# Loading q and k of the first batch in two parts, by halves of the queries, under a newly searched plan

## The chip, the cores and the metric

The kernel runs on one core of one Trainium2 chip. The metric is the device time of one execution in microseconds (us). Engines are named as in the profile: PE (TensorE, matmul), DVE (VectorE), ACT (ScalarE), POOL (GpSimd), SP (SyncE, which issues the DMAs here).

## The reference

Block-causal attention of 8 batches with 8 heads, 576 positions and 64 features, in blocks of 64, and behind it a feed-forward layer on the 4608 tokens:

```python
scores = scale * np.matmul(q, k.transpose(0, 1, 3, 2))
scores = np.where(block_i >= block_j, scores, -1e9)
scores = scores - np.max(scores, axis=-1, keepdims=True)
attn = np.exp(scores)
attn = attn / (np.sum(attn, axis=-1, keepdims=True) + 1e-09)
x = (attn @ v).transpose(0, 2, 1, 3).reshape(B * S, H * D)     # 4608 x 512
h = x @ w_in                                                   # 512 x 2048
sp = np.where(h > 20.0, h, np.log1p(np.exp(np.minimum(h, 20.0))))
out = (h * np.tanh(sp)) @ w_out                                # 2048 x 512
```

q, k and v are float32; w_in and w_out are float64, which the kernel turns into float32 itself from the two 32-bit words of each number.

## The kernel before

**Tiles.** The tokens are worked through in 16 tiles, two per batch. Batch 0 is cut into 384 queries and then 192 (`HALVES[0]`), each later batch in the same two sizes. Heads go in pairs, four pairs per batch. The two products of the feed-forward layer are called fc1 (`m1`, L1597) and fc2 (`m2`, L1702). Most matrix operands are kept as two float16 parts, a high part (`hi`) and the rest (`lo`); three products of parts give one product of the values.

**Batch 0** is loaded by `load_own` (q and k of a pair at L799, v at L811, into `Et`) and is computed in float32 by `attend`: scores by query (`by_query`, L1008 and L1020) only for the largest of each row (DVE, L1038 and L1045), then scores again (L1079), less the largest (L1118), the exponential (L1136, ACT) and the product with v (L1151). Both halves take q and k by `st["A"]`, the list of the loads that they wait for.

**Later batches** are loaded by `load_pair` and split there into parts on DVE, ACT or POOL: `QH`, `KH`, `VH` at L916 and L920, `QL`, `KL`, `VO` at L924. `attend_pair` computes them: scores (L1217, L1229), largest (L1258), exponential (L1292), its parts `P` (L1336, L1342), DMA transposes to `PT`, and the product with v (L1419). `weigh` divides by the sums (L1482, L1483) and splits the result into the parts of x (`xt`; lo at L1510 on DVE), and a DMA transpose (L1552) gives fc1's input `x`.

**Weights.** `weight` loads w_in and w_out in groups (L574), joins the pairs of words on DVE (L583 once and L600 twice per piece), takes sums of squares on ACT, and makes hi (L633 on ACT or L640 on DVE) and lo (L691 on DVE). w_out is staged in `Gt`, the buffer that later holds g, the input of fc2. So `split`, which turns g into hi (L1658 on ACT or L1667 on DVE) and lo (L1673 on DVE), starts for the first tile only when all of w_out has been turned.

**What sets the order.** The program first records all operations with their engines, times and dependences. `Plan.order` then schedules them by a list, each with a due time, and writes them out by planned start. The due times stand in the table `DUE`, with entries for the weights ("w"), the factors of a batch ("batch"), the loads ("load") and the steps of each tile ("tile"). Some casts may go to one of several engines, and the plan picks it. Each engine then runs its instructions in that order.

Of the kernel before, what the change touches and what calls it, by code (L numbers as in the profile page):

```python
# [20 lines left out]
P = 128  # L21
# [11 lines left out]
    "load": (
        (208.5, -15.5, 753.5, -60),
        (11, 400.5, 274, -70.5),
        (340, 173.5, 586.5, 293.5),
        (578, 514, 523.5, 553.5),
        (424.5, 386.5, 195, 638.5),
        (322.5, 411.5, 596, 331),
        (584, 710.5, 581, 634),  # L40
        (438, 791, 455, 590),
        (680, 545.5, 578, 593),
    ),
    "tile": (
        (-224.5, -143.5, 54.5, -83, -49.5, 18.5, -40.5, -39.5,
         390, 274.5, 399.5, 301, 31.5, -9.5, 456.5,
         285.5, 377.5, 60.5, 43.5, 313, 373, 541.5),
# [6 lines left out]
        (556, 28.5, 43.5, 267.5, 271, 246.5, 357, 631,
         78.5, 354.5, 335.5, 437.5, 368.5, -81, 131.5,
         346.5, 484, 458, 450.5, -175.5, 259, -164),
        (499, 409, 666, 287.5, 361.5, 346, 584.5, 335.5,
         410.5, 580.5, 432, 328.5, 456, -17, 480.5,
         803, 688, 639.5, 703, 535, 795.5, 716),
        (375.5, 527, 655.5, 634.5, 283.5, 770, 564.5, 346,  # L60
         425, 319, 858, 637.5, 494.5, 350.5, 351.5,
         929, 577, 311.5, 608.5, 548, 597.5, 159),
        (306.5, 431, 500, 483.5, 571.5, 1003.5, 781.5, 774,
         365, 672, 681.5, 628.5, 660.5, 502.5, 476,
         685, 408, 626.5, 522.5, 753.5, 818.5, 612),
        (433.5, 846, 424.5, 516.5, 719, 718, 500.5, 370.5,
         291, 514, 709.5, 645.5, 739.5, 11.5, 1009.5,
         871.5, 834, 978.5, 960.5, -56, 497.5, 184),
        (439.5, 516, 278.5, 523, 696, 408, 425.5, 656,
         339.5, 783, 867, 642.5, 943, 496, 707.5,  # L70
         635.5, 556.5, 683, 526.5, 854.5, 1014, 576),
        (593.5, 821.5, 469.5, 708, 1061.5, 887, 1110.5, 767.5,
         934, 825.5, 611.5, 831.5, 550.5, 183, 942,
         665, 465, 1008.5, 532, -321, 616, -132.5),
        (795.5, 1021, 1212.5, 461, 796.5, 965, 738, 804.5,
         543.5, 1015, 850.5, 1107.5, 800, 351, 1100,
         641.5, 827, 830, 518.5, 520, 1157, 626),
        (840, 631.5, 963.5, 1028, 1010, 859, 729.5, 885.5,
         715.5, 640, 1192, 1173, 978.5, -42, 1032.5,
         604.5, 1306, 972.5, 1169.5, 147.5, 750.5, -88.5),  # L80
        (1060.5, 775, 744, 721.5, 1067, 849, 818, 691.5,
         706.5, 899.5, 717.5, 943.5, 1099.5, -7.5, 741,
         670, 1056.5, 1241.5, 789.5, 1082.5, 638, 882.5),
        (1025, 1352.5, 1013, 610, 788.5, 728, 1114.5, 1102,
         968.5, 1007, 846, 931, 1091, -24, 740,
         1131.5, 719.5, 1054.5, 854.5, -2.5, 938, 423.5),
# [1785 lines left out]
```

## Time and profile before

| | |
|---|---|
| median of 3 runs | 999.4 us (996.87 to 999.95) |
| the profiled execution | 998.63 us, its span 996.9 us |
| granted PE clock, mean | 0.995 |
| PE busy | 973.1 us (98%) |
| DVE busy | 668.5 us (67%) |
| ACT busy | 663.4 us (67%) |
| POOL busy | 115.0 us (12%) |

The span is what the trace covers; 1.7 us of the execution lie around it. The shares of busy time are means over the whole span: the first 150 us, in which batch 0 is attended to and the weights are turned, differ from the rest. In a row of PE's timeline several instructions of one kind stand together, and a number in brackets is the idle time ahead of them and what ended it. A granted clock of 1.00 is 2.4 GHz, 0.50 is 1.2 GHz.

### The profile page before, as it was taken

The page shows a single profiled execution, that of the slowest core. Times are in us where ns is not written, and L with a number is a line of the kernel's source. Part 1 is how long each engine was busy: PE and PEld are TensorE (multiplying, and loading weights), DVE is VectorE, ACT ScalarE, POOL GpSimd, SP SyncE. Part 2 cuts the span into 40 slices and gives each one's busy share as a digit, 9 for nine tenths or more (in the row PEclk, how much of TensorE's full clock was granted, in tenths as well). Part 3 has the DMA queues.
Part 4 walks back from the last instruction along what each step waited for, and adds up shares of the span by engine and source line. Part 5 has one row for each costly group of instructions (what it writes and reads, how often), then busy time and mean ns, then how long its engine had stood idle before and what let it go on. Part 6 is the DMA issues. An engine that isn't in the chain of part 4 may idle for free.

```text
span 996.9 us, 25050 instructions
## 1 busy us (share of the span) xinstructions
PE 973.1 (98%) x10576; PEld 722.2 (72%) x10576; DVE 668.5 (67%) x1411; ACT 663.4 (67%) x1062; POOL 115.0 (12%) x166
## 2 busy tenths in 40 slices
PE   6999879999999999999999999999999999999998
PEld 5677557786777867777677866777677776876787
DVE  5999999779899687564798378965389636420210
ACT  3769987769768678656788678887668835432221
POOL 0011232011112002000120031010011000000000
PEclk9999979999999999999999999999999999999999
DMA  9863755796677745472668377873277333420000
GB/s 324 270 174 113 183 97 140 152 180 149 119 165 163 163 100 110 91 161 50 143 151 171 71 135 137 156 148 50 57 173 146 76 69 82 82 57 1 25 17 25
DMA packets 275505, 121.56 MB, mean 122 GB/s; under 512 B 221376, under 2 KB 261568, under 8 KB 275392
## 3 DMA queue, kind: packets, MB, share of 16 engines
q1 hardware_dynamic: 275392, 119.97, 55.4%
q8 instruction: 82, 1.34, 0.5%
q14 instruction: 31, 0.25, 0.1%
HBM read 56.10 MB, written 9.44 MB: 66 GB/s over the span
## 4 chain that ended last, share of the span: by engine, by line
PE 86%; DVE 9%; DMA 2%; issue 1%; ACT 1%; SPq 1%; ACTq 0%; DVEq 0%
PE acc L1702 37%; PE acc L1597 35%; PE u L1419 7%; PE ss L1217 6%; DVE Gt L600 1%; DVE wo_h L600 1%; DMA x<-xt 1%; DVE wo_l L691 1%; DMA wo_l<-in_w_in_dram 1%; DVE PT L1045 1%; PE u L1151 1%; DVE pv L1258 1%; DMA PT<-P 1%; DVE P L1342 0%; DVE wi_l L691 0%
## 5 line engine op out<-in xcount | busy, mean ns | idle before, releaser
L1597 PE MATMUL acc<-x,wi_h 128*128 128x192 f16 (+1 forms) x2048 | 394.8, 286 | 4.1 <-ACT Et L1626 2.7
L1702 PE MATMUL acc<-Gt,wo_h 128*128 128x192 f16 (+1 forms) x2048 | 386.1, 287 | 0.2 <-DVE Gt L1673 0.2
L1702 PE MATMUL acc<-Gt,wo_l 128*128 128x192 f16 (+1 forms) x1024 | 293.7, 287 | 0.0
L1597 PE MATMUL acc<-x,wi_l 128*128 128x192 f16 (+1 forms) x1024 | 293.0, 286 | 0.0
L1597 PEld LDWEIGHTS <-wi_h 128*128 128x128 f16 x2048 | 191.1, 98 | 86.0 <-issue 8.5
L1702 PEld LDWEIGHTS <-wo_h 128*128 128x128 f16 x2048 | 187.6, 98 | 50.2 <-issue 3.3
L1626 ACT ACTIVATE Et<-acc,bv 128x384 f32<-128x384 f32 x192 | 109.4, 579 | 118.1 <-PE acc L1597 116.7
L1292 ACT ACTIVATE pe<-ss,pv 128x192 f32<-128x192 f32 (+1 forms) x280 | 148.1, 606 | 12.8 <-DVE pv L1266 8.2
L1673 DVE SCALAR_TENSOR_TENSOR Gt<-Et,bv,Gt 128x1536 f16<-128x1536 f32 (+1 forms) x64 | 91.3, 1432 | 78.7 <-ACT Gt L1658 78.3
L1258 DVE TENSOR_REDUCE pv<-ss 128x2 f32<-128x384 f32 (+4 forms) x140 | 106.0, 789 | 41.8 <-PE ss L1229 41.5
L1702 PEld LDWEIGHTS <-wo_l 128*128 128x128 f16 x1024 | 100.4, 98 | 34.0 <-issue 1.1
L1597 PEld LDWEIGHTS <-wi_l 128*128 128x128 f16 x1024 | 100.2, 98 | 33.1
L1342 DVE TENSOR_TENSOR P<-pe,P 128x256 f16<-128x256 f32 (+1 forms) x168 | 110.8, 700 | 14.9 <-ACT P L1336 13.3
L1292 ACT ACT_TABLE_LOAD x59 | 75.7, 1283 | 12.5 <-DVE pv L1266 7.8
L1336 POOL CAST P<-pe 128x256 f16<-128x256 f32 (+3 forms) x81 | 60.3, 777 | 201.9 <-DMA PT<-P 79.2
L1626 ACT ACT_TABLE_LOAD x62 | 79.5, 1283 | 1.1
L1419 PEld LDWEIGHTS <-PT 128*128 128x128 f16 x2128 | 72.8, 98 | 5.1 <-issue 0.6
L1419 PE MATMUL u<-VH,PT 128*128 128x65 f16 x1344 | 74.3, 193 | 0.0
L1658 ACT ACTIVATE Gt<-Et,bv 128x768 f16<-128x768 f32 (+1 forms) x51 | 63.4, 1248 | 15.9 <-PE acc L1702 14.0
L1419 PE MATMUL u<-VO,PT 128*128 128x64 f16 x784 | 72.6, 193 | 0.0
L1741 ACT ACTIVATE ot<-acc,bv 128x192 f32<-128x192 f32 (+1 forms) x46 | 21.1, 487 | 66.8 <-PE acc L1702 52.9
L1217 PEld LDWEIGHTS <-QH 64*128 64x128 f16 x896 | 27.4, 95 | 28.7 <-issue 13.5
(126 smaller groups left out, 978.7 us busy)
## 6 DMA issues: line engine op xcount, KB each, us to landing
out_dram<-ot SPq DMA_DIRECT2D x48, 192.0 KB, 2.0
wo_l<-in_w_in_dram SPq DMA_DIRECT2D x8, 1024.0 KB, 7.3
Gt<-in_w_out_dram SPq DMA_DIRECT2D x16, 512.0 KB, 4.5
kl<-in_v_dram SPq DMA_DIRECT2D x28, 288.0 KB, 3.1
ql<-in_q_dram SPq DMA_DIRECT2D x28, 288.0 KB, 3.0
kl<-in_k_dram SPq DMA_DIRECT2D x28, 288.0 KB, 3.1
VL<-in_v_dram SPq DMA_DIRECT2D x28, 192.0 KB, 2.9
VL<-in_v_dram SPq DMA_DIRECT2D x28, 96.0 KB, 3.1
```

What stands on the lines that cost most here:

```text
L1217: nc.tensor.matmul(ss[:, 512 * a + col : 512 * a + col + n], lhsT=m[q_][hs, at : at + P], rhs=m[k_][hs, key : key + n], start=first, stop= ...
L1258: nc.vector.reduce_max(out=mx[:, c], in_=ss[:, :, c0:c1], axis=mybir.AxisListType.X)
L1292: nc.scalar.activation(pe[ex[r].slot][:, cols], ss_[S0[r].slot % NSS][:, cols], AF.Exp, scale=esc, bias=mx[:, c, a : a + 1],)
L1336: op(out=h, in_=x)
L1342: nc.vector.tensor_sub(l, x, h)
L1419: nc.tensor.matmul(out, lhsT=p_, rhs=v_, start=first, stop=True, skip_group_check=True,)
L1597: nc.tensor.matmul(pt, lhsT=w[:, d, f * P : (f + 1) * P], rhs=x[:, d, :], start=k == 0 and d == 0 and z == 0, stop=d == NP - 1 and z == 2, ...
L1626: nc.scalar.activation(Et[:, (self.i * NG + g) % NE, j : j + K, 0:n], acc_[c.slot % NACC][:, 0 : K * n].rearrange("p (k n) -> p k n", k=K) ...
L1658: lambda g_hi=g_hi, ev=ev: nc.scalar.activation(g_hi, ev, AF.Copy, scale=self.s_g),
L1673: lambda g_hi=g_hi, g_lo=g_lo, ev=ev: nc.vector.scalar_tensor_tensor(out=g_lo, in0=ev, scalar=self.s_g, in1=g_hi, op0=ALU.mult, op1=ALU.su ...
L1702: nc.tensor.matmul(pt, lhsT=w[:, f, o * P : (o + 1) * P], rhs=g, start=k == 0 and f == 0 and z == 0, stop=f == NF - 1 and z == 2, skip_gro ...
L1741: evac(lambda o, i, s: nc.scalar.activation(o, i, AF.Copy, scale=s))
```

## The change

`load_own` issues two transfers for q and two for k of each pair of batch 0: columns 0 to 384 (the first half of the queries and the keys that they see) and columns 384 to 576. The second part carries a due time of its own, the first entry of the pair in tile 1. `attend` waits in the first half for the first parts only, and in the second for both. v is loaded as before. The whole table `DUE` is new, so that the order on every engine is another one.

```diff
-    "w": ((-53.5, -7.5, 92, 14.5), (645, 263, 668.5, 387)),
+    "w": ((-85, 131, 174, 350.5), (416, 560.5, 362.5, 233.5)),
...
-        ins = [
-            add(
-                "sp",
-                dma(P * S * 4),
-                lambda t=t, src=src: nc.sync.dma_start(out=t, in_=src),
-            )
-            for t, src in ((m["QF"], qT[0, rows]), (m["KF"][:, 0:S], kT[0, rows]))
-        ]
+        parts = []
+        for h, (c0, c1) in enumerate(HALVES[0]):
+            plan.part("load", 0, p)
+            if h:
+                plan.part("tile", 1, 2 * p)
+            parts.append(
+                [
+                    add(
+                        "sp",
+                        dma(P * (c1 - c0) * 4),
+                        lambda t=t, src=src, cs=slice(c0, c1): nc.sync.dma_start(
+                            out=t[:, cs], in_=src[:, cs]
+                        ),
+                    )
+                    for t, src in ((m["QF"], qT[0, rows]), (m["KF"], kT[0, rows]))
+                ]
+            )
+        plan.part("load", 0, p)
...
-        return {"m": m, "A": ins, "C": v_ins, "u": ([], [])}
+        return {"m": m, "A": (parts[0], parts[0] + parts[1]), "C": v_ins, "u": ([], [])}
...
-            S1 = add("pe", (us + 0.2, us * 2400), by_query, st["A"] + rooms)
+            S1 = add("pe", (us + 0.2, us * 2400), by_query, st["A"][half] + rooms)
...
-        S0 = add("pe", (us + 0.2, work), scores, st["A"] + rooms)
+        S0 = add("pe", (us + 0.2, work), scores, st["A"][half] + rooms)
```

Behind `load_own` a line of the program has a number higher by 11 than before (L1038 is L1049 now, L1673 is L1684); lines 799 and 811 are L806 and L822.

**SP, the first loads.** `in_q_dram` and `in_k_dram` are q and k, `in_w_in_dram` is w_in. Before, from the loads of v to those of pair 2:

```order
L811 DMA Et<-in_v_dram 64x128 x3
L799 DMA Et<-in_q_dram 128x576
L799 DMA Et<-in_k_dram 128x576
L574 DMA wo_l<-in_w_in_dram 128x2x1024 x2
L799 DMA Et<-in_q_dram 128x576
L799 DMA Et<-in_k_dram 128x576
```

Now, from the first halves of pair 3 (those of pairs 1 and 2 stand ahead of them in the same way):

```order
L806 DMA Et<-in_q_dram 128x384
L806 DMA Et<-in_k_dram 128x384
L806 DMA Et<-in_q_dram 128x192
L806 DMA Et<-in_k_dram 128x192
L574 DMA wo_l<-in_w_in_dram 128x2x1024 x2
L806 DMA Et<-in_q_dram 128x192
L806 DMA Et<-in_k_dram 128x192
L574 DMA Gt<-in_w_out_dram 128x4x256 x2
```

The first halves of all four pairs, and the second half of pair 0, moved ahead of the first two pieces of w_in; before, pairs 0 and 1 as wholes stood there.

**DVE, around the first piece of w_in.** `acc` is a PSUM bank with the scores of batch 0, `PT` holds the largest of each row, `wo_h` and `wo_l` stage w_in. Before:

```order
L750 TENSOR_SCALAR bv_114<-bv_114 128x1
L583 TENSOR_SCALAR wo_h<-wo_l 128x1024
L600 SCALAR_TENSOR_TENSOR wo_h<-wo_l,wo_h 128x1024 x2
L1038 TENSOR_REDUCE PT_96<-acc_135 128x1
L1038 TENSOR_REDUCE PT_96<-acc_136 128x1
```

Now:

```order
L750 TENSOR_SCALAR bv_114<-bv_114 128x1
L1049 TENSOR_REDUCE PT_96<-acc_135 128x1
L1049 TENSOR_REDUCE PT_96<-acc_136 128x1
L1049 TENSOR_REDUCE PT_96<-acc_135 128x1
L1049 TENSOR_REDUCE PT_96<-acc_136 128x1
L583 TENSOR_SCALAR wo_h<-wo_l 128x1024
L600 SCALAR_TENSOR_TENSOR wo_h<-wo_l,wo_h 128x1024
```

The four maxima of pair 1 moved from behind the first piece of w_in to ahead of it.

**DVE, around the first split of g.** `Et` holds g, `Gt` its parts; `P`, `pe` and `tt` belong to the attention of batch 1. Before:

```order
L924 SCALAR_TENSOR_TENSOR KL_72<-kl,pv_113,KH_71 128x576
L1463 TENSOR_SCALAR dv_119<-u_133 128x6
L1673 SCALAR_TENSOR_TENSOR Gt<-Et,bv_114,Gt 128x1536
L1342 TENSOR_TENSOR P_94<-pe_123,P_94 128x2x3x128
L1342 TENSOR_TENSOR P_94<-pe_123,P_94 128x2x2x64
L1482 RECIPROCAL dv_119<-dv_119 128x6
L1483 TENSOR_TENSOR tt_121<-u_133,dv_119 128x384
L1673 SCALAR_TENSOR_TENSOR Gt<-Et,bv_114,Gt 128x1536
```

Now:

```order
L691 SCALAR_TENSOR_TENSOR wo_l<-Gt,wo_s,wo_h 128x16x128
L1269 TENSOR_REDUCE pv_112<-ss_132 128x2
L1274 TENSOR_TENSOR pv_112<-pv_112 64x2
L1275 COPY pv_112<-pv_112 64x2
L1277 TENSOR_SCALAR pv_112<-pv_112 128x4
L1678 TENSOR_SCALAR Gt<-Et,bv_114 128x1536
L1684 SCALAR_TENSOR_TENSOR Gt<-Et,bv_114,Gt 128x1536 x4
L768 TENSOR_SCALAR bv_114<-wo_s,bv_114 128x4
```

The four low parts of the first tile's split stand in one row now, with the first high part on DVE right ahead of them; before, two steps of the attention and more stood between one low part and the next.

**PE, where fc2 begins.** `ss` is a bank of scores, `far_q` and `far_k` constants of the mask. Before, the end of the block of scores and the start of fc2:

```order
L1229 LDWEIGHTS far_q
L1229 MATMUL ss_131<-far_k,far_q 128x64
L1702 LDWEIGHTS wo_h
L1702 MATMUL acc_136<-Gt,wo_h 128x384
L1702 LDWEIGHTS wo_h
L1702 MATMUL acc_136<-Gt,wo_h 128x384
```

Now:

```order
L1608 LDWEIGHTS wi_l
L1608 MATMUL acc_136<-x_128,wi_l 128x192
L1713 LDWEIGHTS wo_h
L1713 MATMUL acc_134<-Gt,wo_h 128x384
L1713 LDWEIGHTS wo_h
L1713 MATMUL acc_134<-Gt,wo_h 128x384
```

The block of scores (22 products of pair 2 in batch 1) moved behind 48 products of fc2. What stands ahead of them now is 42 products of fc1 (tile 1), 66 of values (L1430) and 6 more of fc1; before, fc1's last products stood ahead of the 66 of values, and fc2 began with runs of 12 products between runs of fc1.

## Rows read from the trace of the kernel before

**Rows 1.** Stretches of the span: length, busy time of each engine, granted clock, DMA share, GB/s.

```profile
0.00:50.00 50.00, 41.05 (x319) 30.25 (x320) 38.26 (x97) 27.32 (x47) 3.99 (x15) 1.00 0.91 297
...
100.00:150.00 50.00, 40.56 (x408) 26.77 (x407) 49.24 (x92) 44.75 (x66) 16.47 (x15) 0.90 0.67 139
...
150.00:950.00 800.00, 800.00 (x8957) 590.23 (x8955) 529.20 (x1120) 540.51 (x877) 86.56 (x125) 1.00 0.56 115
```

**Rows 2.** PE's timeline ahead of fc2: start, length, instructions, idle time before them.

```profile
127.14 0.33 PE L1597 MATMUL acc<-x,wi_h 128*128 128x192 f16 x2
...
131.10 0.19 PE L1419 MATMUL u<-VH,PT 128*128 128x65 f16 x1
...
137.95 0.61 PE L1217 MATMUL ss<-KH,QH 64*128 64x128 f16 x6 [4.69 <-DVE KH L920]
...
140.37 0.61 PE L1217 MATMUL ss<-KL,QH 64*128 64x128 f16 x6 [1.82 <-DVE KL L924]
...
142.17 0.48 PE L1702 MATMUL acc<-Gt,wo_h 128*128 128x384 f16 x1 [0.22 <-DVE Gt L1673]
```

**Rows 3.** The chain that ended last, up to 146 us: start, length, piece.

```profile
7.40 7.24 DMA wo_l<-in_w_in_dram
...
140.39 1.74 DVE Gt L1673
```

**Rows 4.** Stretches from the first weights to the first split, and around fc2's start.

```profile
14.67:140.39 125.72, 111.15 (x1056) 81.26 (x1057) 120.82 (x248) 98.37 (x146) 22.61 (x26) 0.98 0.67 187
...
125.80:136.04 10.24, 7.45 (x124) 6.77 (x121) 9.93 (x22) 9.76 (x18) 4.36 (x4) 1.00 0.39 39
...
136.04:146.28 10.24, 6.29 (x38) 3.44 (x39) 10.10 (x20) 8.71 (x10) 3.54 (x3) 0.50 0.58 124
```

**Rows 5.** The stretch in which the first weights land.

```profile
10.00:20.00 10.00, 9.03 (x75) 7.26 (x73) 6.27 (x16) 4.19 (x11) 0.44 (x1) 1.00 1.01 387
```

**Rows 6.** DVE's timeline, three places.

```profile
24.75 1.42 DVE L1038 TENSOR_REDUCE PT<-acc 128x1 f32<-128x384 f32 x4 [0.47 <-PE acc L1020]
...
46.19 1.29 DVE L1045 TENSOR_REDUCE PT<-ss 128x2 f32<-128x896 f32 x2 [0.62 <-PE ss L1020]
...
110.60 0.41 DVE L1510 TENSOR_TENSOR xt<-tt,xt 128x256 f16<-128x256 f32 x1
```

**Rows 7.** SP's timeline, q and k of pair 1.

```profile
6.30 0.58 SPq L799 DMA_DIRECT2D Et<-in_q_dram  x1
...
6.93 0.43 SPq L799 DMA_DIRECT2D Et<-in_k_dram  x1
```

**Rows 8.** DVE by line and form: shapes, count, busy us, mean ns, idle before.

```profile
L640 DVE TENSOR_SCALAR wo_h<-Gt,wo_s 128x2048 f16<-128x2048 f32 x2 | 3.1, 1564 | 0.0
...
L1336 DVE CAST P<-pe 128x1024 f16<-128x1024 f32 x15 | 10.9, 724 | 6.6 <-DMA PT<-P 4.6 <-issue 1.9
...
L920 DVE TENSOR_SCALAR KH<-kl,pv 128x576 f16<-128x576 f32 x19 | 10.1, 533 | 0.0
...
L1667 DVE TENSOR_SCALAR Gt<-Et,bv 128x1536 f16<-128x1536 f32 x7 | 7.5, 1066 | 42.4 <-PE acc L1702 37.1 <-ACT Et L1626 5.4
...
L920 DVE TENSOR_SCALAR QH<-ql,pv 128x512 f16<-128x512 f32 x15 | 7.8, 520 | 0.0
...
L920 DVE TENSOR_SCALAR QH<-ql,pv 128x128 f16<-128x128 f32 x15 | 6.0, 402 | 0.0
...
L924 DVE SCALAR_TENSOR_TENSOR VO<-VL,bv,VH 128x512 f16<-128x512 f32 x28 | 20.9, 745 | 0.0
...
L924 DVE SCALAR_TENSOR_TENSOR VO<-VL,bv,VH 64x256 f16<-64x256 f32 x28 | 15.9, 569 | 0.0
```

**Rows 9.** PE's timeline, a block of scores and what follows it.

```profile
96.71 0.40 PE L1217 MATMUL ss<-KH,QH 64*128 64x128 f16 x6
...
97.54 1.67 PE L1151 MATMUL u<-Et,pe 128*128 128x65 f32 x13
```

**Rows 10.** The transposes of x by their line.

```profile
DMA to landing us min/median/max: 2.8/4.3/9.8
```

More of the change, by code (lines that the diff above doesn't have):

```diff
@@ L30 @@
 DUE = {
-    "w": ((-53.5, -7.5, 92, 14.5), (645, 263, 668.5, 387)),
-    "batch": (150.5, 378.5, 470, 303.5, 451.5, 828.5, 524.5, 841.5),
+    "w": ((-85, 131, 174, 350.5), (416, 560.5, 362.5, 233.5)),
+    "batch": (50.5, 94, 577, 447.5, 765.5, 1054, 577.5, 1107.5),
     "load": (
[L34 to L42, printed above, removed]
+        (355, 377, 774.5, -36),
+        (-73.5, 348, 491, -147),
+        (380.5, 866, 620.5, 441),
+        (700, 437, 410.5, 386.5),
+        (549, 595, 491, 444),
+        (425, 482, 574, 300.5),
+        (542, 676, 537.5, 646),
+        (457, 869.5, 446.5, 499),
+        (682.5, 521.5, 598.5, 629.5),
@@ L54 @@
[L54 to L83, printed above, removed]
@@ L84 @@
[L84 to L92 removed]
+        (-250, -171, 346.5, -110.5, -100, 254, -121, -16,
+         737.5, 307, 442, 274, 258, -224.5, 447,
+         511, 553, 378, 36.5, 358.5, 411, 333.5),
@@ new lines @@
+        (327.5, -94, -9.5, 755.5, 475.5, -19.5, 522.5, 509,
+         207.5, 757.5, 995, 293, 438.5, 235.5, 371,
+         905.5, 377, 731.5, 560.5, -44.5, 625.5, -48),
+        (401.5, 563, 554.5, 585, 136.5, 579, 588, 479,
+         261.5, 297.5, 796, 278, 354.5, 466, 507.5,
+         372.5, 162, 471.5, 761.5, 773, 643.5, 304),
+        (716, 40.5, 704.5, 484.5, 232, 247.5, 361, 639.5,
+         91.5, 482, 541.5, 446, 480.5, 96, 393.5,
+         610.5, 543, 721.5, 663.5, -98, 261, 79),
+        (338, 692, 903, 393.5, 472, 534, 611.5, 550.5,
+         225, 550.5, 656, 305, 533, 54, 529.5,
+         633, 643, 633, 947, 580.5, 769.5, 753.5),
@@ new lines @@
+        (638, 548, 718.5, 570, 293.5, 627, 665, 181,
+         471, 693, 683, 410, 459, 287.5, 336,
+         789.5, 712.5, 422, 727, 668.5, 557, -93.5),
+        (547, 377, 769, 689, 742, 1068, 925.5, 704.5,
+         438.5, 435, 397, 446, 311, 327, 523,
+         531.5, 997.5, 610, 608, 799, 793.5, 468.5),
+        (821.5, 726, 863, 639, 296, 446, 1204.5, 490.5,
+         444, 474, 886, 401, 660.5, -84, 555,
+         988, 1043, 941.5, 1042, -72.5, 662, 317.5),
+        (352.5, 1241.5, 300, 397, 684.5, 318, 454, 523.5,
+         350.5, 1085.5, 1101.5, 602, 736, 509, 791,
+         706.5, 870, 429, 428.5, 618, 1131, 819.5),
@@ new lines @@
+        (530, 837.5, 1172.5, 1119, 559.5, 1037.5, 665.5, 529.5,
+         1081.5, 615, 1008, 931, 469, -42, 590.5,
+         1063, 516, 1079.5, 607, -205.5, 679, -112.5),
+        (509, 1004.5, 609.5, 566, 967, 549, 931, 781,
+         506.5, 958, 816, 815, 712.5, 343, 1064.5,
+         727.5, 967.5, 720.5, 1058, 678.5, 909.5, 946.5),
+        (699, 731, 1253, 1137, 505.5, 824.5, 605, 1037.5,
+         866.5, 1050, 883.5, 1256, 601.5, -169.5, 1025.5,
+         618, 1382.5, 1312, 1285, 339, 903.5, -119.5),
@@ new lines @@
+        (1359.5, 1152, 1312, 699.5, 1233, 1055, 648, 1197,
+         934, 829.5, 795.5, 865.5, 1000.5, 57, 1056.5,
+         615, 1179.5, 991.5, 925.5, 1262.5, 824.5, 669.5),
+        (1128, 1122.5, 489, 826, 873, 665.5, 671, 990.5,
+         486.5, 929.5, 1005.5, 961, 874, -173.5, 1052,
+         1025.5, 741.5, 1133.5, 1153.5, -139.5, 1610.5, 499),
+        (869.5, 1103, 744, 1089, 1102, 1065, 701.5, 1366.5,
+         879, 1229.5, 1170, 1042, 772, -154.5, 1096,
+         724.5, 994, 806.5, 675.5, 1066, 1167.5, 1185.5),
@@ L93 @@
+        (891.5, 1027, 591, 1031.5, 824, 1338, 638, 1250,
+         911.5, 899, 1166, 869, 963.5, -70, 1212.5,
+         1061.5, 1250.5, 1222.5, 1489.5, 540, 1581, 647),
     ),
```

15 lines of the change are left out of this document (removed).

## The prediction

> **What bounds the kernel now.** I read the stretches of the span first, to see where TensorE (PE) is not busy. It is idle for 50.00 − 41.05 = 8.95 us in the first 50 us and for 50.00 − 40.56 = 9.44 us between 100 and 150 us; from 150 to 950 us it is busy for 800.00 of 800.00 us [rows 1]. So behind some point X the end is fixed: X, plus the PE work that is left at X. A change can only move X, move PE work from one side of X to the other, or put a new wait behind X.
>
> PE's timeline finds X. Before the first fc2 products stand 4.69 us of waiting for the high part of a K (L920) and 1.82 us for its low part (L924), and the last wait is the one of 0.22 us for the first split of g (L1673), which ends at 142.17; no wait follows [rows 2]. The chain of waits gives what is late in front of it: the first piece of w_in lands at 7.40 + 7.24 = 14.64, and the chain ends in the split that starts at 140.39 [rows 3]. Between, the Vector engine (DVE) is busy for 120.82 of 125.72 us [rows 4]. So X = arrival of the first weights + all DVE work that the order puts ahead of the first low part of a split + that part itself. Nothing else that the change does counts unless it is on this line: ScalarE has 98.37 us of work in the same stretch, GpSimd 22.61 [rows 4].
>
> **The change, part by part.**
>
> *1. The first weights come later.* The new order issues, ahead of the first piece of w_in, q and k of the first half for all four pairs and of the second half for pair 0: 8 × 192 KB + 2 × 96 KB = 1728 KB, where 4 × 288 KB = 1152 KB stood. That is 576 KB more, 0.59 MB, on DMA engines that are full: share 1.01, 387 GB/s [rows 5]. 0.59 MB / 387 GB/s = 1.5 us. The first q and k are 192 KB smaller, so PE may start about 0.5 us sooner; that is hidden, since X hangs on DVE. Against the 1.5 us, the four maxima of pair 1 now stand ahead of the first weight on DVE, where DVE would otherwise idle; they take 1.42 us (the row of pair 2's four, of the same tile) [rows 6]. Net +0.1 us. Bounds: −0.4 if the half microsecond of the smaller first pair reaches the weights too, and +1.6 if issuing is the limit: six issues more at (7.40 − 6.30) / 2 = 0.55 us are 3.3 us [rows 3, 7], of which 1.42 + 0.3 are covered.
>
> *2. DVE has other work ahead of the first split.* I counted the instructions ahead of the first L1673 (L1684 now) in both orders; durations are from [rows 8]. Gone from there: one high part of w_out (−1.56, ScalarE has it now), one cast of P (−0.72), one low part of x (−0.41 [rows 6]), one high part of K (−0.53). Added: the first split's own high part on DVE (+1.07), two pairs of casts of Q (2 × (0.52 + 0.40) = +1.84) and one pair of low parts of V (0.74 + 0.57 = +1.31). Sum: +4.22 − 3.22 = +1.0, and a few small factors less: +0.9. Each is DVE time on the line that sets X, so it counts in full. Bounds +0.4 and +1.4, since means of a form hide its spread.
>
> *3. Idle time of DVE.* On the way to X it waited 0.47 us for maxima's products and 0.62 us for others of batch 0 [rows 6]. Both waits are for PE's attention on batch 0, whose inputs come in another order now. I take half away: −0.5 (bounds −1.09 and 0).
>
> *4. PE work that changes sides.* In the trace a block of scores of pair 2 stands right ahead of the first L1702; the new order puts it behind 48 of them. A block of that size takes 97.54 − 96.71 = 0.83 us [rows 9]. It filled time in which PE starved, and now comes at PE's own rate after X: +0.8 us (bounds 0 and +0.8; 0 if PE reaches X late anyway). Everything else ahead of X on PE is the same work in another order, inside PE's idle time.
>
> *5. PE's clock.* In the stretch from 125.80 the granted clock is 1.00 with 7.45 us busy, in the next, from 136.04 to 146.28, 0.50 with 6.29 us busy; there the lower level of 1.2 GHz holds to the end of the stretch [rows 4]. fc2 began at 142.17, so 146.28 − 142.17 = 4.11 us ran at half speed, a loss of 2.05 us. The new order has fc2 behind two idle stretches of PE (below), so the fall stays likely, and it may be longer: +0.5 (bounds −2.05 and +2.05).
>
> *6. Behind X.* The four splits of the first tile now stand in one row on DVE, 1.74 us each [rows 3], and what stood among them comes later, such as the input of the next tile. PE had no wait there before, and the nearest wait of this kind is 1.82 us [rows 2]. I take +0.2 (bounds 0 and +1.8).
>
> Table loads, GpSimd's share and the split of the transfers in itself cost nothing on the line: SP has time between issues once the first 15 us are over, and ScalarE has slack ahead of X.
>
> **Sum:** 0.1 + 0.9 − 0.5 + 0.8 + 0.5 + 0.2 = +2.0 us on the profiled execution, 998.63 → 1000.6. The median of the runs shown, 999.4, is 0.8 above that execution, so the time is 1001.4.
>
> **Rivals.**
>
> *a. The lower clock takes hold before X (slower).* The fourth low part of x for tile 1's input stood on DVE at 110.60 [rows 6]; in the new order 127.0 us of DVE work stand ahead of it in place of 109.8, so it comes near 127, and its DMA transposes land 2.8 to 9.8 us later, mostly 4.3 [rows 10]: near 132. Until then PE has nothing, since the products that filled its time there in the trace (127.14 to 131.10: 48 products in 3.96 us [rows 2]) now wait for that input. What is left for PE between 132 and X is 48 products of fc1 (3.9 us) and 66 of values (131.10 to 137.95 − 4.69 = 133.26, 2.2 us), 6.1 us at full speed and 12.2 at half. PE would then stand idle for about 3 us less than it needs: 1001.4 + 6.1 − 3 = 1004.5. It decides from the granted clock between 131 and 140: at 1.00 nothing happens, at 0.50 it does. For it: one idle stretch of 4.69 us was enough in the trace. Against it: the 13 us from 131 to X hold even the slow products. The Trainium skill, "TensorE: Matmul & The Clock Gate", section "What's actually happening", has the throttled level as the default, which activity releases, and the phase as free-running; by that rule two idle stretches would make this rival likelier than I have it, and differ from run to run. The trace shows the fall once.
>
> *b. The first weights are bound by the issue of small parts (slower).* If each part costs SP's 0.55 us whatever its size, w_in is issued at 10.7 in place of 7.40 and lands at 17.9, if it keeps its 7.24 us [rows 3, 7]. DVE then starts 1.7 us later than in my sum: 1003.1. Against it: the queue was full at that time, so the 7.24 us are mostly waiting in line behind bytes, which later issue shortens. The Trainium skill, "DMA: Bandwidth & Descriptors", section "Rules for kernel authors", says to coalesce many small transfers into a large one, which speaks against the change; the parts of 96 and 192 KB are above the 64 KB under which it sees mostly overhead, and the share of 1.01 [rows 5] shows no gaps that more transfers would widen.
>
> *c. The gains all come, the losses don't (faster).* The weights come half a microsecond sooner (−0.4 for part 1), both DVE waits vanish (−1.09), the clock stays at 1.00 (−2.05), nothing is late behind X: −0.4 + 0.9 − 1.09 + 0.8 − 2.05 = −1.8 on the profiled execution: 997.6. For it: the first q and k are smaller. Against it: the DVE work ahead of X grew, and that is counted, not guessed. To be faster than 996.4 another 1.2 us is needed, such as most of parts 2 and 4 being hidden.
>
> *d. The change does nothing that reaches X:* the moved work is all covered. 999.4.
>
> **How the numbers follow.** A measurement here can tell about 0.3% from no change, 3.0 us: faster is below 996.4, slower above 1002.4. The forecast as summed: 0.42, of which a quarter (0.10) ends above 1002.4 by its bounds. Rival a 0.16 (0.13 of it above 1002.4), b 0.12 (0.08), c 0.20 (0.10 below 996.4, with the DVE terms at their low ends too), d 0.10 (0.03 below). Faster 0.14, slower 0.31, same 0.55. The likeliest is the sum, 1001.4. Its own bounds, with terms that do not all fall on one side, are 998.5 to 1004; rival a reaches 1004.5, c 997.6 and, with the DVE terms low, 996.4. The range is 996.4 to 1005.
>
> **What would show it.** Landing of the first w_in piece near 16.2 (part 1; 17.9 for b). Start of the first low part of a split near 141 and first fc2 product near 143 to 144 (parts 1 to 3). The pair's score block behind the fc2 products, with no wait (part 4). Granted clock 0.50 in the stretch that holds X, 1.00 in the one before (a: 0.50 in both). PE without a wait from 150 us on (part 6). The forecast is wrong if DVE reaches the split before 140 or after 143, or if PE waits again behind X, at the next tile's input.

## The result and the profile after

| | before | after |
|---|---|---|
| median of 19 runs each, taken side by side | 998.28 us (995.77 to 999.95) | 1002.19 us (996.96 to 1006.68) |
| the profiled execution | 998.63 us, span 996.9 us | 1005.27 us, span 1003.2 us |
| granted PE clock, mean | 0.995 | 0.994 |

The ratio is 1.0044, 95% interval 1.0029 to 1.0058: the change makes the kernel slower by 3.9 us of the medians. The profiled execution of after is 3.1 us above its median and that of before 0.4, so what is read from the two traces (6.3 us of span) holds some 2.7 us that are this execution's own. One run of a_two below, at a mean granted clock of 0.655, took 1438.67 us and is left out of that kernel's numbers.

The stretches of after, columns as in [rows 1]; the fourth row runs from the start of DVE's work on the way to X to the first low part of a split, as in [rows 4]:

```profile
0.00:50.00 50.00, 44.85 (x324) 34.07 (x326) 34.50 (x91) 23.30 (x39) 5.74 (x17) 1.00 0.83 269
100.00:150.00 50.00, 40.95 (x368) 25.35 (x368) 49.17 (x88) 44.09 (x65) 12.27 (x16) 0.90 0.64 146
150.00:950.00 800.00, 797.40 (x8992) 591.56 (x8991) 536.32 (x1150) 526.15 (x875) 75.63 (x101) 1.00 0.57 115
16.06:142.96 126.90, 118.42 (x1049) 85.62 (x1050) 120.93 (x250) 90.90 (x133) 22.78 (x27) 0.97 0.65 189
```

PE is busier in the first 50 us than before (44.85 against 41.05) and the kernel is slower: many of its early products run at half rate. DVE has less done there, 34.50 against 38.26. And from 150 us on PE is no longer busy all the time.

PE's timeline of after, at the places that answer to [rows 2], and behind X (start, length, instructions, idle time before and what ended it):

```profile
121.26 0.80 PE L1608 MATMUL acc<-x,wi_h 128*128 128x384 f16 x2 [2.37 <-ACT Et L1637]
...
135.93 0.34 PE L1608 MATMUL acc<-x,wi_h 128*128 128x192 f16 x2 [2.22 <-DMA x<-xt]
...
142.42 0.33 PE L1713 MATMUL acc<-Gt,wo_h 128*128 128x384 f16 x1
144.73 0.32 PE L1713 MATMUL acc<-Gt,wo_h 128*128 128x384 f16 x1 [1.99 <-DVE Gt L1684]
...
154.14 0.40 PE L1228 MATMUL ss<-KH,QH 64*128 64x128 f16 x6
...
154.97 0.34 PE L1608 MATMUL acc<-x,wi_h 128*128 128x192 f16 x2
...
232.78 0.48 PE L1608 MATMUL acc<-x,wi_h 128*128 128x384 f16 x2 [0.92 <-ACT Et L1637]
...
238.72 0.49 PE L1608 MATMUL acc<-x,wi_h 128*128 128x384 f16 x2 [1.46 <-ACT Et L1637]
```

X is still the first low part of a split: the product of fc2 that needs it starts at 144.73, where before it started at 142.17. That is +2.56 of the 6.3 us. The other 3.7 lie behind X: the block of scores that stood ahead of fc2 runs from 154.14 to 154.97 now, and PE waits twice more for the activation of fc1's output (L1637).

How X came late, from the other end. SP's timeline of after (start, length, issue), against [rows 7] and the `7.40 7.24` of [rows 3]:

```profile
6.30 0.58 SPq L806 DMA_DIRECT2D Et<-in_q_dram  x1
6.93 0.43 SPq L806 DMA_DIRECT2D Et<-in_k_dram  x1
...
7.93 0.38 SPq L806 DMA_DIRECT2D Et<-in_k_dram  x1
9.38 0.33 SPq L806 DMA_DIRECT2D Et<-in_q_dram  x1
...
10.70 0.43 SPq L806 DMA_DIRECT2D Et<-in_k_dram  x1
11.17 0.94 SPq L574 DMA_DIRECT2D wo_l<-in_w_in_dram  x2
```

The landing of that piece, from the issues of the 0.4 us around it:

```profile
wo_l<-in_w_in_dram SPq DMA_DIRECT2D x1, 1024.0 KB, 5.8
```

The first piece of w_in is issued at 11.17 in place of 7.40 and lands near 11.17 + 5.8 = 17.0 in place of 14.64. Two stretches of DMA (last two columns: share, GB/s), of after:

```profile
8.00:12.00 4.00, 3.40 (x21) 2.51 (x17) 0.93 (x3) 2.27 (x5) 0.00 (x0) 1.00 0.98 280
12.00:16.00 4.00, 3.53 (x25) 2.59 (x24) 0.68 (x5) 2.13 (x6) 0.44 (x1) 1.00 0.96 337
```

and of before:

```profile
8.00:12.00 4.00, 3.83 (x20) 2.94 (x21) 1.24 (x5) 2.50 (x7) 0.00 (x0) 1.00 0.94 319
12.00:16.00 4.00, 4.00 (x41) 3.49 (x39) 1.98 (x7) 1.90 (x4) 0.44 (x1) 1.00 1.01 392
```

The engines are as full as before and move 12 and 14% less. DVE's timeline of after in this stretch:

```profile
16.06 1.42 DVE L1049 TENSOR_REDUCE PT<-acc 128x1 f32<-128x384 f32 x4 [2.41 <-PE acc L1031]
17.39 0.68 DVE L583 TENSOR_SCALAR wo_h<-wo_l 128x1024 int32<-128x1024 int32 x1
...
21.77 0.19 DVE L1493 RECIPROCAL dv<-dv 128x6 f32<-128x6 f32 x1 [2.43 <-ACT dv L1467]
...
27.11 1.42 DVE L1049 TENSOR_REDUCE PT<-acc 128x1 f32<-128x384 f32 x4 [1.37 <-PE acc L1031]
...
142.87 7.56 DVE L1684 SCALAR_TENSOR_TENSOR Gt<-Et,bv,Gt 128x1536 f16<-128x1536 f32 x4
```

In this execution DVE does not wait for the first weight: it takes it at 17.39 right behind four maxima, which had waited 2.41 us for PE. It waits twice for PE's products (2.41 and 1.37 us) and once for ACT (2.43 us), which reads the 24 value products that follow, of after and of before:

```profile
15.96 5.38 PE L1162 MATMUL u<-Et,pe 128*128 128x65 f32 x24
```

```profile
14.57 2.89 PE L1151 MATMUL u<-Et,pe 128*128 128x65 f32 x24
```

### The profile page after: what moved, and what is told of

Read it like the earlier page. It is cut to its first block, busy times and chain, and to the rows that moved or that the text cites. A ratio compares the mean times of both kernels' runs of the same rounds, so it can differ in the third digit from the quotient of the medians.

```text
span 1003.2 us, 25033 instructions
## 1 busy us (share of the span) xinstructions
PE 981.2 (98%) x10576; PEld 727.4 (73%) x10576; DVE 672.9 (67%) x1434; ACT 640.1 (64%) x1047; POOL 104.0 (10%) x142
## 4 chain that ended last, share of the span: by engine, by line
PE 83%; DVE 10%; issue 2%; ACT 2%; DMA 2%; SPq 0%; POOL 0%; ACTq 0%; DVEq 0%; POOLq 0%
PE acc L1713 34%; PE acc L1608 33%; PE u L1430 6%; PE ss L1228 5%; PE u L1162 1%; DVE Gt L600 1%; DVE pv L1269 1%; DVE wo_h L600 1%; DMA kl<-in_k_dram 1%; DVE PT L1056 1%; ACT pe L1303 1%; DVE wo_l L691 1%; DVE P L1353 1%; PE acc L1019 1%; DMA PL<-P 1%
## 5 line engine op out<-in xcount | busy, mean ns | idle before, releaser
L1637 ACT ACTIVATE Et<-acc,bv 128x384 f32<-128x384 f32 x192 | 109.8, 579 | 127.8 <-PE acc L1608 126.6
L1684 DVE SCALAR_TENSOR_TENSOR Gt<-Et,bv,Gt 128x1536 f16<-128x1536 f32 (+1 forms) x64 | 92.1, 1444 | 113.3 <-ACT Gt L1669 112.9
L1269 DVE TENSOR_REDUCE pv<-ss 128x2 f32<-128x384 f32 (+4 forms) x140 | 106.0, 789 | 16.6 <-PE ss L1240 16.3
L1430 PEld LDWEIGHTS <-PT 128*128 128x128 f16 x2128 | 73.0, 98 | 5.5 <-DMA PT<-P 0.5
L1430 PE MATMUL u<-VH,PT 128*128 128x65 f16 x1344 | 74.5, 193 | 0.4 <-DMA PT<-P 0.4
L1430 PE MATMUL u<-VO,PT 128*128 128x64 f16 x784 | 72.7, 193 | 0.0
L1669 ACT ACTIVATE Gt<-Et,bv 128x768 f16<-128x768 f32 (+1 forms) x47 | 57.1, 1220 | 13.9 <-PE acc L1713 12.8
L1515 POOL CAST xt<-tt 128x384 f16<-128x384 f32 (+1 forms) x38 | 32.9, 865 | 310.5 <-DVE tt L1494 298.2
L1752 ACT ACTIVATE ot<-acc,bv 128x384 f32<-128x384 f32 (+1 forms) x40 | 18.9, 499 | 69.6 <-PE acc L1713 62.3
L1347 POOL CAST P<-pe 128x256 f16<-128x256 f32 (+3 forms) x48 | 41.4, 894 | 139.2 <-DVE P L1353 46.2
```

Of the source, the lines that this page charges most:

```text
L1269: nc.vector.reduce_max(out=mx[:, c], in_=ss[:, :, c0:c1], axis=mybir.AxisListType.X)
L1347: op(out=h, in_=x)
L1430: nc.tensor.matmul(out, lhsT=p_, rhs=v_, start=first, stop=True, skip_group_check=True,)
L1515: ("pool", elem(nqc * P), lambda: nc.gpsimd.tensor_copy(out=th, in_=tx)),
L1637: nc.scalar.activation(Et[:, (self.i * NG + g) % NE, j : j + K, 0:n], acc_[c.slot % NACC][:, 0 : K * n].rearrange("p (k n) -> p k n", k=K) ...
L1669: lambda g_hi=g_hi, ev=ev: nc.scalar.activation(g_hi, ev, AF.Copy, scale=self.s_g),
```

## The experiments

Theory B: the weights come late, DVE and PE then wait for each other, and this delays X. Rival A: PE itself starts slowly (its products at half rate up to 24 us), through the order of batch 0's small inputs. Rival C: the new order of DVE's work. Apart from them, what stands behind X. In the edits `move(a, b)` puts recorded operation a right ahead of operation b in the finished order, and `warm(i, n, bank)` puts n products of 384 columns, whose results nobody reads, ahead of operation i. All times are medians of 11 or 12 runs (b_late_warm: 6), each ratio is against the kernel before, run beside it: its median was 997.45 us beside the first four kernels, 997.56 beside the next four and 997.03 beside the last four. A trace is of one execution. The first four runs:

**a_pair0_whole.** After, with the second parts of pair 0's q and k right behind the first part of q.

```diff
+    move(6, 5)
+    move(7, 5)
```

> The changed kernel in its own order, with one thing taken back: the second parts of q and k of pair 0 are issued between the first part of q and the first part of k, so that PE gets its first operands as late as in the kernel before. Theory A (PE's slow start): in the changed kernel's trace PE starts at 3.79 in place of 4.71, stands still for 1.07 us at 12.47, and its products run at about half speed until about 24 (24 products of values take 5.38 us, 2.89 before), so that DVE waits 2.41, 2.43 and 1.37 us for it. With PE started later the pause is gone, the values take 2.9 us again and DVE's three waits shrink to about 2.5 us together: 2 to 3 us less than the changed kernel, near 999.5. Theory B (the weights come later, as in part 1 of the prediction): nothing changes, 1002 within 1 us, since the weights still stand behind the same bytes.

1000.76 us, ratio 1.0026 (1.0007 to 1.0046): the interval overlaps that of after and takes in what either theory expects. The first 24 value products run at full rate here, the next 24 do not, and the weights come later still (PE's timeline, then DVE's):

```profile
26.99 5.33 PE L1162 MATMUL u<-Et,pe 128*128 128x65 f32 x24
```

```profile
19.86 0.69 DVE L583 TENSOR_SCALAR wo_h<-wo_l 128x1024 int32<-128x1024 int32 x1 [2.94 <-DMA wo_l<-in_w_in_dram]
```

**a_identity_early.** After, with the identity matrix made earlier, which PE waited for at 12.47 (1.07 us).

```diff
+    move(1, 28)
+    move(3, 28)
```

> The changed kernel in its own order, with one thing moved: the scaled identity that the first subtraction (L1129) waits for is made on ACT ahead of the sums of squares of v, so PE does not wait 1.07 us for it at 12.47; PE still starts early. Theory A1 (the pause keeps PE slow): the values take 2.9 us in place of 5.38 and the time falls by 2 to 3 us, to about 999.5. Theory A2 (the early start itself does it): PE stays slow until about 24 and the time falls by less than 1 us. Theory B (late weights): no change.

1001.94 us, 1.0041 (1.0023 to 1.0059). PE's pause is gone and its first 24 value products are at full rate, but the time is that of after. PE's timeline:

```profile
13.19 2.89 PE L1162 MATMUL u<-Et,pe 128*128 128x65 f32 x24
...
22.43 0.82 PE L1129 MATMUL ss<-PT,PT 128*128 128x128 f16 x6 [4.22 <-DVE PT L1062]
...
25.91 5.33 PE L1162 MATMUL u<-Et,pe 128*128 128x65 f32 x24
```

Rival A falls as the whole cause: with a fast start PE runs ahead and then stands 4.22 us for DVE, which waits 4.06 us for w_in, landed at 18.78; behind that wait PE's products are at half rate again.

**b_two_dmas.** Before in its own order, each load of q and k as two transfers.

```diff
-                lambda t=t, src=src: nc.sync.dma_start(out=t, in_=src),
+                lambda t=t, src=src: [
+                    nc.sync.dma_start(out=t[:, c], in_=src[:, c])
+                    for c in (slice(0, Q0), slice(Q0, S))
+                ],
```

> The kernel before in its own order, but each load of q and of k of batch 0 is issued as two transfers, 384 and 192 columns, one right behind the other at the same place: the split alone. If the split of the transfers costs nothing by itself (part of the prediction): 0 within 1 us of the kernel before, about 998.3, and the first weights land within 1 us of 14.64. If parts are bound by their issue (rival b): four more issues ahead of w_in at 0.55 us, landing up to 2.2 us later and the time up to 2.2 us longer. If PE's early start alone makes it slow (theory A2): PE starts before 4.7, its products stay at half speed past 14 and the time is 1 to 3 us longer.

998.27 us, 1.0000 (0.9986 to 1.0013). The split alone brings the first weights to DVE at 16.31, 1.6 us late, and X has made up for most of it by the end:

```profile
140.85 1.80 DVE L1676 SCALAR_TENSOR_TENSOR Gt<-Et,bv,Gt 128x1536 f16<-128x1536 f32 x1
```

Up to there DVE idles 3.59 us where before it idled 4.90.

**a_weights_first.** After, with the first two pieces of w_in ahead of the first halves of pairs 2 and 3 and the second half of pair 0.

```diff
+    move(34, 16)
+    move(38, 16)
```

> The changed kernel in its own order, with the first two pieces of w_in issued ahead of the first parts of pairs 2 and 3 and the second part of pair 0. Part 1 of the prediction (the bytes ahead of w_in cost 1.5 us): the first piece lands about 2.5 us sooner than in the changed kernel. If X hangs on that, the time falls by 1 to 2 us. Theory A (DVE's first maxima of pair 1 wait for PE at 16.06, and DVE takes the weights only behind them): less than 0.5 us.

999.58 us, 1.0006 (0.9989 to 1.0024), 3.8 us less than after by the ratios, whose intervals are apart; by the medians, each against the kernel before beside it, it is 1.8 us less (+2.1 in place of +3.9). The stretch from DVE's first maxima of pair 1 to the first low part of a split:

```profile
14.23:138.76 124.53, 115.36 (x1049) 83.97 (x1050) 120.82 (x250) 91.04 (x134) 23.50 (x27) 0.96 0.68 196
```

DVE idles 124.53 − 120.82 = 3.71 us. Two issues in another place take between half of the loss (medians) and nearly all of it (ratios) away: B, and not the plan's order of DVE's work (C), which is as in after; the upper end of the interval leaves C and all else 2.4 us. X, at 138.76, is 1.6 us sooner than before and the time is not: what the new plan loses behind X (the block of scores, and waits for L1637) stays.

The next four ask for each mechanism alone.

**b_weights_late.** Before, with the first two pieces of w_in issued behind the loads of pairs 2 and 3: nothing else of the change.

```diff
+    move(26, 587)
+    move(30, 587)
```

> The kernel before in its own order, with whole loads, and only the first two pieces of w_in moved behind q and k of pairs 2 and 3. It does to the kernel before what the new order does with its first loads, and nothing else of the change. Theory B (late first weights are the main cost): 1152 KB stand ahead that stood behind, about 3 us at 387 GB/s; the first piece lands near 17.5 and the time rises by 2 to 4 us, to 1000 to 1002. Theory P (the plan's other moves are the cost: work on DVE ahead of the split, the scores behind fc2, waits behind X): DVE finds other work meanwhile and the time stays within 1 us of the kernel before.

1000.52 us, 1.0033 (1.002 to 1.0046). Late weights alone, in the order of before, make some three quarters of the loss by the ratios. DVE's and PE's timelines:

```profile
17.45 0.69 DVE L583 TENSOR_SCALAR wo_h<-wo_l 128x1024 int32<-128x1024 int32 x1 [3.89 <-DMA wo_l<-in_w_in_dram]
...
21.84 0.79 PE L1008 MATMUL acc<-Et 64*128 64x256 f32 x1 [4.05 <-DVE PT L1038]
...
29.43 5.38 PE L1151 MATMUL u<-Et,pe 128*128 128x65 f32 x24
...
146.98 1.80 DVE L1673 SCALAR_TENSOR_TENSOR Gt<-Et,bv,Gt 128x1536 f16<-128x1536 f32 x1
```

and the stretch behind PE's wait:

```profile
21.84:37.51 15.67, 15.67 (x86) 13.10 (x88) 10.57 (x27) 6.25 (x10) 0.40 (x1) 0.50 0.71 238
```

Before, the same stretch reads:

```profile
21.84:37.51 15.67, 13.96 (x127) 11.04 (x128) 14.79 (x34) 10.99 (x18) 0.64 (x1) 1.00 0.87 277
```

The weight is 2.8 us late and the split 6.7 in this execution, the slowest of the 11; the median of the times is 3.0 us above that of before. DVE, whose maxima stood behind the weight, holds up PE for 4.05 us; PE's granted clock is 0.50 (1.2 GHz) for the next 15.67 us; and DVE, waiting for those products, does 10.57 us of work where it did 14.79.

**b_dve_more.** Before, with the last low part of w_out (L691) computed twice: 2.2 us more on DVE.

```diff
+    op[342].emit = lambda f=op[342].emit: (f(), f())
```

> The kernel before in its own order, with the last low part of w_out (L691, 2.26 us in the chain) computed twice by DVE ahead of the first split. If DVE's work ahead of X sets the end at full price, as parts 1 to 3 of the prediction hold: +2.2 us, about 999.7 where the kernel before has 997.5, and the first fc2 products near 144.4. If PE or the clock sets X instead: less than 1 us.

999.32 us, 1.0010 (0.9995 to 1.0025); the first low part of a split starts at 143.14, 2.8 us later. The direction is as the model of X has it, and the interval takes in both 0 and 2.2 us: whether DVE's work counts in full is not settled.

**b_warm.** Before, with 41 unread products ahead of the block of scores at 137.95.

```diff
+    warm(711, 41, lambda: ss_[op[710].slot % NSS])
```

> The kernel before in its own order, with 41 products of 384 columns, whose results nobody reads, put into PE's idle time ahead of the block of scores that waits for KH at 137.95. They fill 133.1 to about 139.8. If the fall of the granted clock from 136 to 146 costs 2.05 us (part 5 of the prediction): the stretch that holds X is at 1.00 and the time falls by about 2 us, to 995.5, faster than both kernels. If the clock falls in any case, or something else is late at once: within 0.5 us.

997.63 us, 1.0004 (0.999 to 1.0019). The stretch that read 0.50 in [rows 4]:

```profile
136.04:146.28 10.24, 9.20 (x85) 6.21 (x84) 10.21 (x14) 8.44 (x11) 4.92 (x3) 1.00 0.57 113
```

The clock is up at 2.4 GHz, the profiled execution 2.1 us faster, the median not. So no gain from the clock at X could be measured; by the interval it is 1.0 us at most.

**a_behind_x.** After, to take PE's waits behind X away: a piece of V's load stands ahead of the two DMA transposes of x and P that it stood behind on SP, and one activation of L1637 ahead of two sums of squares (L874) on ACT.

```diff
+    move(1172, 796)
+    move(806, 1267)
```

> The changed kernel in its own order, with two things moved that stand behind X: the last load of v of a pair of batch 2 ahead of the transpose of x that is issued before it (223.24 in the trace), and one Mish on ACT ahead of the sums of squares that wait for q (230.70). In the changed kernel PE waits 0.92 and 1.46 us for Mish at 232.78 and 238.72 (part 6 of the prediction, +0.2 there with a bound of 1.8). If ACT's waits for these loads cause them: PE has at most one of the two waits left behind X, and the time falls by 1 to 2.4 us, to about 1000. If DVE or the transposes are late anyway: within 0.5 us of the changed kernel, 1002.

1000.75 us, 1.0027 (1.0011 to 1.0042): 0.7 us less than after by the medians, each against the kernel before beside it, and 1.7 by the ratios, whose intervals overlap. The wait in question (total, times, longest), of after and of this kernel:

```profile
PE acc L1608 <- ACT Et L1637: 2.4, 2, 1.5
```

```profile
PE acc L1608 <- ACT Et L1637: 0.8, 1, 0.8
```

1.6 us of waiting went; whether as much of the time did is open. This run shows something else too. Its order up to X is that of after, and its execution went otherwise (PE's timeline, then DVE's):

```profile
15.70 2.89 PE L1162 MATMUL u<-Et,pe 128*128 128x65 f32 x24
```

```profile
19.21 0.70 DVE L583 TENSOR_SCALAR wo_h<-wo_l 128x1024 int32<-128x1024 int32 x1 [1.99 <-DMA wo_l<-in_w_in_dram]
...
140.24 7.56 DVE L1684 SCALAR_TENSOR_TENSOR Gt<-Et,bv,Gt 128x1536 f16<-128x1536 f32 x4
```

The first weight comes 1.8 us later than in after's execution, the value products run at full rate, and X is 2.6 us sooner, as soon as in before. So the +2.56 us at X in after's trace belongs to executions with slow products, and not to the order alone.

The last four ask whether late weights cost through the clock, and whether a better version exists.

**b_late_warm.** b_weights_late, with 26 unread products (of zeros) in PE's wait of 4.05 us.

```diff
+    nc.vector.memset(wi_h[:, 0, 0:Q0], 0.0)
+    warm(126, 26, lambda: ss_[op[128].slot % NSS])
```

> The kernel with the first weights late (the kernel before in its own order, w_in's first two pieces behind q and k of pairs 2 and 3), and 26 products of 384 columns, whose results nobody reads, ahead of the maxima's products for which PE waited 4.05 us at 21.84. In the late kernel's trace the granted clock is 0.50 from about 21 to 38, products take twice as long, and DVE then waits 2.46 and 2.23 us for them. Theory C (late weights cost by way of PE's clock): the clock stays at 1.00, those waits shrink to about 1 us together and the time falls by 1.5 to 2.5 us, to 998 to 999. Theory L (it is the lateness itself): the time stays at 1000.5 within 0.7.

1003.39 us, 1.0049 (1.0031 to 1.0066): no faster than b_weights_late, whose interval overlaps. PE's timeline, then a row of DVE's:

```profile
15.80 5.38 PE L1151 MATMUL u<-Et,pe 128*128 128x65 f32 x24
...
20.98 6.07 PE L1848 MATMUL ss<-wi_h 128*128 128x384 f16 x26
```

```profile
27.73 0.76 DVE L1038 TENSOR_REDUCE PT<-acc 128x1 f32<-128x256 f32 x2 [3.13 <-PE acc L1020]
```

PE was slow before the added products here, which then ran for 6.07 us and held up the maxima. The clock was 1.00 after that, but the run doesn't tell lateness from clock.

**a_two.** a_weights_first and a_behind_x together.

> The changed kernel in its own order with two things taken back at once: w_in's first two pieces ahead of the first parts of pairs 2 and 3, and the moves behind X (one load of v ahead of a transpose of x, one Mish ahead of two sums of squares). Alone they took 0.38% and 0.17% off the changed kernel, against a loss of 0.44%. If the two are independent, a ratio of 0.999 to the kernel before, about 996.5. If they hide each other: about 1.000 to 1.0006, as with the weights alone.

998.41 us, 1.0017 (0.9998 to 1.0036). The waits behind X fell to 0.4 us, but no sum of the two gains can be seen. The stretch in which this profile differs:

```profile
13.64:23.88 10.24, 10.24 (x52) 8.68 (x54) 5.85 (x15) 2.06 (x4) 0.00 (x0) 0.50 0.93 309
```

PE is at 1.2 GHz there, in the stretch in which batch 0 starts; the 24 value products at 15.53 took 5.38 us. The interval overlaps that of a_weights_first nearly whole.

**a_all.** a_two, with DVE's high part of the first split (L1678) behind the first two low parts instead of ahead of them, and 13 unread products between a block of scores and fc1 of tile 1, and 13 between fc1 and the first fc2.

```diff
+    move(437, 438)
+    warm(515, 13, lambda: acc_[op[515].slot % NACC])
+    warm(441, 13, lambda: acc_[op[441].slot % NACC])
```

> The same as the kernel with both moves, and besides: the high part of the first tile's split that DVE makes ahead of the first low part is made behind the second low part (part 2 of the prediction: 0.93 us of DVE's line, so X 0.9 sooner), and 13 products of 384 columns whose results nobody reads stand ahead of tile 1's fc1 and 13 ahead of the first fc2, where PE waited 2.1 us each (part 5: the clock at X stays at 1.00, 1 to 2 us). If both hold: 1.5 to 2.5 us less than without them, 994 to 995, faster than both kernels. If the clock was not worth anything there: 0.9 less.

997.36 us, 0.9997 (0.9981 to 1.0012). The loss is gone; nothing is gained over before.

**b_start.** Before, with the identity earlier, 9 unread products ahead of the first scores, and the 41 of b_warm.

```diff
+    move(1, 20)
+    move(3, 20)
+    nc.vector.memset(wi_h[:, 0, 0:Q0], 0.0)
+    warm(101, 9, lambda: acc_[op[99].slot % NACC])
+    warm(711, 41, lambda: ss_[op[710].slot % NSS])
```

> The kernel before in its own order with three additions: 9 products of 384 columns of zeros on PE ahead of its first scores, while q and k are on their way; the scaled identity on ACT ahead of the sums of squares; and the 41 products ahead of the block of scores that waits for KH at 137.95. If PE's products at half speed until about 13 are what DVE's early waits hang on: the scores take 1.14 us in place of 2.08 from the start, and the time falls by 1 us beside the 2.2 us that the profile with the 41 products alone showed, to 994 to 995. If the weights' arrival at 14.64 covers all that: as with the 41 products alone, 997.6 by the median.

996.99 us, 1.0006 (0.9989 to 1.0022): no gain. DVE's first weight stays where it was:

```profile
14.54 0.69 DVE L583 TENSOR_SCALAR wo_h<-wo_l 128x1024 int32<-128x1024 int32 x1 [0.94 <-DMA wo_l<-in_w_in_dram]
```

No version beats the kernel before by more than its interval.

## Why the prediction was right or wrong

**The number and the side.** 1001.4 was forecast and 1002.19 measured. With before at 998.28 in the runs taken side by side, that is +3.9 where +2.0 was summed. The direction held; the summed size was half of what came. That the number is so near is in part luck: it started from 999.4, 1.1 us too high, and added 1.9 too little. "Within 0.3%", to which the prediction gave its largest chance, is not what happened: 0.44% slower was given 0.31. (Its chance of faster adds up to 0.13 from its own parts, not 0.14.) The sum came near with three of its terms much too small and two too large. All six, from the two profiled executions:

| part | forecast | measured | from |
|---|---|---|---|
| 1 first weights | +0.1 | +1.4 | DVE's run to X starts at 14.67 → 16.06 |
| 2 DVE's work | +0.9 | +0.1 | busy 120.82 → 120.93 |
| 3 DVE's idle time | −0.5 | +1.1 | 4.90 → 5.97 |
| 4 block of scores | +0.8 | +0.8 | 154.14 to 154.97, behind X |
| 5 clock at X | +0.5 | −0.2 | half rate behind X until about 148.5; before until about 146.2 |
| 6 waits behind X | +0.2 | +2.4 | 0.92 + 1.46 |

They make 5.6 of 6.3 us. The first three are of one execution: a_behind_x, with the same order up to X, had none of their sum.

*Part 1 failed in its rate.* It let the 576 KB more run at the 387 GB/s of [rows 5]. That row holds the large weight transfers; the stretch in which the small parts move had 280 to 337 GB/s in after. Issue came on top: from 6.30 on SP took 4.87 us for the eight parts ahead of w_in, 0.37 to 0.63 us apart but for a pause between 7.93 and 9.38. Rival b forecast issue at 10.7 and landing at 17.9; it was 11.17 and 17.0, and 19.2 in a_behind_x, whose issues stand in the same order. In after's execution DVE did not wait for the piece, since its start at 16.06 hung on PE's slow products; in a_behind_x it did, for 1.99 us. So b's mechanism was there, and its time of 1003.1 is as near to the measured one as the forecast; it had a chance of 0.12. The Trainium skill, "DMA: Bandwidth & Descriptors", section "Rules for kernel authors", says to coalesce many small transfers. The trace agrees, and further up than the 64 KB below which the page sees mostly overhead: with parts of 96 and 192 KB 12 to 14% less was moved, and b_two_dmas, which only cuts the transfers in two, moved 338 GB/s from 10 to 20 us where before moved 387. The prediction set that sentence aside by the share of 1.01, and the share was the wrong witness: it stayed at 0.96 to 0.98 while the bytes fell.

*Part 3 failed in its sign.* It took waits of before and asked how much of them would go. The runs show that DVE and PE are coupled in the first 40 us: a DVE that is late with maxima stops PE, PE goes on at half rate, and DVE waits for it. X is the start of DVE's run + busy + idle, and the busy part hardly moves: 120.6 to 121.2 us in all executions but a_all (119.9) and b_dve_more (123.1). All fourteen executions, by the rate of batch 0's value products in the first 40 us (2.8 to 3.1 us for 24 of them, or 5.3 and more). Times are in us, X as in the chain of waits, where it stands 0.1 us later than in the timeline:

| kernel | first weight | slow value products from | DVE idle | X | ratio of the runs |
|---|---|---|---|---|---|
| b_warm | 14.4 | none | 3.5 | 138.6 | 1.0004 |
| a_weights_first | 15.6 | none | 3.7 | 138.8 | 1.0006 |
| b_start | 14.5 | none | 3.5 | 139.0 | 1.0006 |
| a_all (0.9 us less work) | 16.9 | none | 3.8 | 139.3 | 0.9997 |
| a_behind_x | 19.2 | none | 3.9 | 140.3 | 1.0027 |
| before | 14.7 | none | 4.9 | 140.4 | |
| b_two_dmas | 16.3 | none | 3.6 | 140.9 | 1.0000 |
| b_dve_more (2.2 us more work) | 14.6 | none | 5.5 | 143.2 | 1.0010 |
| a_two | 17.0 | 15.5 | 5.2 | 141.6 | 1.0017 |
| after | 17.4 | 16.0 | 6.0 | 143.0 | 1.0044 |
| b_late_warm | 17.4 | 15.8 | 6.9 | 145.3 | 1.0049 |
| a_identity_early | 18.8 | 25.9 | 11.0 | 145.3 | 1.0041 |
| b_weights_late | 17.5 | 29.4 | 8.6 | 147.1 | 1.0033 |
| a_pair0_whole | 19.9 | 27.0 | 11.0 | 147.7 | 1.0026 |

The price of lateness is not its length: with the first weight 1.6 us late in the trace nothing could be measured, with 2.8 us late the medians rose by 3.0, and a_pair0_whole, 5.2 us late, has a ratio below that of after. What goes with X in these executions is the rate of PE's products: wherever they were slow, X was at 141.6 or later, wherever not, at 140.9 or sooner, but for the one kernel with more work for DVE. Where they fell from full to half rate, PE had just stood 3.08 to 4.22 us for DVE (a_pair0_whole, b_weights_late, a_identity_early); in after, a_two and b_late_warm they were slow from the start. Shown is that late weights are enough (b_weights_late) and that between half and nearly all of the loss goes with them (a_weights_first). That the step between runs through PE's clock is argued from these traces, one execution each, and was not told apart by a run: b_late_warm, meant for it, was slow from its start.

*Part 2* counted 1.0 us more work for DVE, from means over the whole kernel. Ahead of X the same moved groups add 3.9 us and take 3.5 away, +0.3: the casts of Q and the low parts of V were shorter there than their means (2.85 us in place of 3.15), the high part of w_out longer (1.85 for 1.56). *Part 4* was right, in place and in size. *Part 5* held in place, and b_warm shows that it matters less than the bounds of ±2.05: clock up at X, no median gained. *Part 6* failed by its nearest row. It priced waits by those ahead of X and thought only of the next tile's input; the waits that came are for fc1's activation on ACT, at 232.78 and 238.72, far from the rows that the prediction had looked at. Its upper bound of 1.8 was 0.6 short. It named this failure among its signs ("if PE waits again behind X"), and a_behind_x got 0.7 to 1.7 us back there, though the interval leaves it unproved.

**Rival a** did not come at its place. Three stretches of after, the third column from the end being the granted clock:

```profile
118.00:128.00 10.00, 7.63 (x54) 4.02 (x53) 9.97 (x14) 6.53 (x11) 4.08 (x4) 0.83 0.64 181
128.00:142.00 14.00, 11.43 (x179) 9.07 (x177) 13.72 (x35) 13.56 (x17) 2.47 (x5) 1.00 0.70 141
142.00:148.50 6.50, 4.51 (x23) 2.38 (x20) 6.50 (x6) 6.47 (x11) 1.60 (x1) 0.74 0.67 89
```

From 128 us to X, where the rival wanted 0.50, the clock is 2.4 GHz; the stretches with the waits at 121.26 and 144.73 fall below it. The rule that the prediction set beside rival a (throttled by default, released by activity, from "TensorE: Matmul & The Clock Gate" of the Trainium skill, "What's actually happening", with a phase that runs free) fits what the runs show at another place: the same 24 value products took 5.38 us at 15.80 in b_late_warm and 2.89 at 14.27 in b_weights_late, and 5.38 at 15.96 in after and 2.89 at 15.70 in a_behind_x, where in each two PE's order is the same up to there.

## What to carry to other kernels

A load that is split to let one engine start sooner delays whatever stands behind it in the queue (the split alone: the first weights by 1.6 us); look there first, and move the transfer that the bounding engine needs ahead of the parts. Where two engines feed each other, the cost of a late input is not its length (here nothing for 1.6 us, 3.0 us for 2.8), so price it by putting the input late in the old kernel, not by bytes over a rate. Take more than one trace of a kernel before a cause is read from one: two executions of one order differed by 2.6 us at X. And look for new waits over the whole kernel: those that came here stood 90 us behind the point that the sum was built on.
